# The gate of the first dense layer computed as m(2t - m) on DVE, its high part written by ScalarE

## The chip, the cores and the metric

The kernel runs on one core of a Trainium2 chip. The metric is device time in microseconds (us) of one execution. The engines are called as in the profile: PE (TensorE, matmul), PEld (its weight loads), DVE (VectorE), ACT (ScalarE), POOL (GpSimd) and SP (SyncE, which issues all DMAs of this kernel). Each takes its instructions in a fixed order and waits on semaphores for the others.

## The reference, cut to what matters

Attention over 4 batches, 8 heads, 1152 rows and 64 columns, with neighbouring query rows averaged, then two dense layers on its 2304 rows of 512. The first of them has the gate that is changed:

```python
h = x @ w_in                                   # 2304 x 2048
g = np.where(h >= 1, h, np.where(h <= -1, 0.0, (h + 1) ** 2 / 4))
y = g @ w_out                                  # 2304 x 512
```

The second takes the maximum of three products of y and multiplies it by a last matrix. With t = max(0, h/2 + 1/2) and m = min(t, 1) the gate is g = t^2 where t is at most 1, and 2t - 1 above; both kernels use that.

## The kernel before

**Split numbers.** Matmuls run in float16 on pairs: a float32 array is scaled and written as a high part and a low part (what the rounding left), and a product takes three matmuls (high-high, high-low, low-high). Whoever writes a pair writes the high part first and then the low part from the float32 array and the high part. For the gate that is `g[:, 0]` and `g[:, 1]`.

**Units of attention.** The loop goes over 48 units (b, i, p): batch, third of the 576 query rows, pair of heads. A unit has three score tiles ("who" 0, 1, 2): scores `sc` on PE (L352), the maximum `st` on DVE (L366), scale (L367) and exp `pf` on ACT (L368). Tiles 0 and 1 are split into `hl` (ACT L421, DVE L422) and turned by DMA; tile 2 is turned on PE (`tr`, L404) and split from there (ACT L410, DVE L411). PE then multiplies with V (`av`, L440), and DVE scales the sum into `xf` (L453). Batch 0 is done without these splits.

**Loads of attention.** Every second unit loads and prepares the queries of the next two (`q_prep`): a DMA into `qn`, an add on POOL (L321), square and scale, a split (POOL L245, DVE L246), transposes. Around a change of batch the units also prepare K and V of the next batch: squares on ACT (L266), splits `kpre` and `vhl` (POOL L245, then DVE L246 of 128x1152).

**Dense work between.** From unit 6 on every unit also does four steps of `dense_steps`: two tiles of `up_steps` (ph on PE, L506, then the gate) and one of `down_steps` (py on PE, L532). A gate tile is 128x384 float32, that is 128 of the 2048 columns twice for 192 rows; there are 3 x 4 x 8 = 96 of them. A gate tile before:

```python
nc.scalar.activation(out=t2, in_=ph, func=AF.Relu, scale=hh, bias=0.5)             # L511 ACT
# L512 DVE: rl = max(t, 1) - 1        L513 POOL: rl = t + rl
# L514 DVE: t2 = min(t, 1) * rl       L515 POOL: g high = gs * t2
# L517 DVE: g low = gs * t2 - g high
```

PE reads g only after all eight tiles of a (b, i) have been written, so in the loop there is a unit or more between a gate tile and its use. The tiles t2 and rl have two buffers each.

**What sets the order.** During attention PE's order is the one in which the program is written (`tc.manual_schedule`); DVE, ACT, POOL and SP get theirs from the scheduler, which may interleave dense and attention work. After attention (from about 852 us) PE's order too is the scheduler's. There the last gate tiles stand beside the preparation of the second layer's weights (`st_m`, `wm`: DVE L156 to L161, ACT L664, L147), of which POOL does a part once (L672, L673, 128x2304). The second layer follows until the end.

Of the kernel before, what the change touches and what calls it, by code (L numbers as in the profile page):

```python
# [11 lines left out]
AF = mybir.ActivationFunctionType  # L12
ALU = mybir.AluOpType
# [38 lines left out]
def body(ctx: ExitStack, tc: tile.TileContext, q, k, v, w_in, w_out, w1, w2, w3, w_o2, out):  # L52
    nc = tc.nc
# [416 lines left out]
    def scales(b):  # L470
        hu = small.tile([P, 1], F32, tag="hu", name=f"hu{b}")
        hh = small.tile([P, 1], F32, tag="hh", name=f"hh{b}")
        nc.vector.tensor_scalar(out=hu, in0=U_in[:, 1:2], scalar1=Uv[b][:, NPAIR:NPAIR + 1],
                                scalar2=None, op0=ALU.mult)
        nc.vector.tensor_scalar(out=hh, in0=Uv[b][:, NPAIR + 1:NPAIR + 2], scalar1=0.5, scalar2=None, op0=ALU.mult)

        gd = small.tile([P, 1], F32, tag="dgd", name=f"dgd{b}")
        gs = small.tile([P, 1], F32, tag="dgs", name=f"dgs{b}")
        nc.vector.tensor_scalar(out=gd, in0=hu, scalar1=2.0 ** 31, scalar2=1.0, op0=ALU.mult, op1=ALU.max)
        nc.vector.tensor_scalar(out=gd, in0=gd, scalar1=2.0 ** -15, scalar2=None, op0=ALU.mult)  # L480
        nc.vector.reciprocal(out=gs, in_=gd)
        dst[b] = hh, gd, gs
# [3 lines left out]
    def acc(x, name):  # L486
        ps, tag = room[x]
        return ps.tile([P, 512], F32, tag=tag, name=name)

    def up_steps(b, i):  # L490

        if i == 0:
            scales(b)
        hh, gd, gs = dst[b]
        x = xh.pop((b, i))
        g = gp.tile([P, 2, NF, NB], F16, tag="g", name=f"g{b}_{i}")
        gt[b, i] = g
        for f2 in range(NF // 2):
            key = f"{b}_{i}_{f2}"
            fs = slice(2 * f2, 2 * f2 + 2)  # L500
            ph = acc("h", "ph" + key)[:, :2 * NB].rearrange("p (a n) -> p a n", a=2)
            for a in range(2):
                ff = 2 * f2 + a
                for kt in range(KD):
                    for e, (wi, xi) in enumerate(((0, 0), (0, 1), (1, 0))):
                        nc.tensor.matmul(ph[:, a], win[:, wi, kt, ff * P:(ff + 1) * P], x[:, xi, kt],  # L506
                                         start=(kt == 0 and e == 0), stop=(kt == KD - 1 and e == 2))

            t2 = room["t2"].tile([P, 2, NB], F32, tag="t2", bufs=room["n"], name=f"t2_{key}")
            rl = room["t2"].tile([P, 2, NB], F32, tag="rl", bufs=room["n"], name=f"rl_{key}")  # L510
            nc.scalar.activation(out=t2, in_=ph, func=AF.Relu, scale=hh, bias=0.5)  # L511
            nc.vector.tensor_scalar(out=rl, in0=t2, scalar1=1.0, scalar2=-1.0, op0=ALU.max, op1=ALU.add)  # L512
            nc.gpsimd.tensor_tensor(out=rl, in0=t2, in1=rl, op=ALU.add)  # L513
            nc.vector.scalar_tensor_tensor(out=t2, in0=t2, scalar=1.0, in1=rl, op0=ALU.min, op1=ALU.mult)  # L514
            nc.gpsimd.tensor_scalar(out=g[:, 0, fs, :], in0=t2, scalar1=gs, scalar2=1.0,  # L515
                                    op0=ALU.mult, op1=ALU.mult)
            nc.vector.scalar_tensor_tensor(out=g[:, 1, fs, :], in0=t2, scalar=gs, in1=g[:, 0, fs, :],  # L517
                                           op0=ALU.mult, op1=ALU.subtract)
            yield
# [20 lines left out]
    def dense_steps(units):  # L540

        down = iter(())
        for b, i in units:
            for k, _ in enumerate(up_steps(b, i)):
                yield
                if k % 2 == 1:
                    next(down, None)
                    yield
                    yield
            down = down_steps(b, i)  # L550
        for _ in down:
            yield
            yield
# [299 lines left out]
```

## Time and profile before

| | before |
|---|---|
| time, median of 2 runs | 1233.24 us (1231.83 to 1234.66) |
| time of the profiled execution | 1239.84 us |
| its span | 1237.9 us |
| busy: PE, DVE, ACT, POOL | 1077.9, 857.5, 696.8, 302.9 us |
| POOL L513 and L515 (the gate) | 103.7 and 70.7 us, 96 instructions each |
| chain that ended last: PE, DVE, POOL, DMA | 41%, 17%, 4%, 7% of the span |

The page has five parts that are read here: busy time by engine, 40 slices of the span, the chain of waits that ended last, groups of instructions by line, and DMA issues. By the slices the run has five stretches: up to about 170 us weights and the first batch, without dense work; to 300 us the rest of batch 0; to 840 us attention with dense work; to 950 us the end of the first dense layer beside the next layer's weights; then the second layer, in which PE is full (283 of 288 us) and nothing of the gate runs.

### The profile page before, as it was taken

What the parts mean: (1) busy time and instruction counts of PE and PEld (TensorE: products, weight loads), DVE (VectorE), ACT (ScalarE), POOL (GpSimd) and SP (SyncE); (2) the same over time, 40 slices, a digit from 0 to 9 for tenths busy, and PEclk for the clock granted to TensorE, in tenths of its full rate; (3) what the DMA queues carried; (4) which work ended last, traced back from release to release, by engine and by line L of the source; (5) the groups of instructions that cost most, each with busy time, mean ns of one, the idle gap of its engine ahead of it and who ended that gap; (6) DMA issues with size and microseconds to landing.
All of it is one profiled execution on the core that took longest, in us unless ns stands there. A gap on an engine that the chain in (4) does not pass through costs nothing.

```text
span 1237.9 us, 26735 instructions
## 1 busy us (share of the span) xinstructions
PE 1077.9 (87%) x11058; PEld 881.2 (71%) x11058; DVE 857.5 (69%) x1454; ACT 696.8 (56%) x1241; POOL 302.9 (24%) x306
## 2 busy tenths in 40 slices
PE   0456788899999987999988899998697999999998
PEld 0334567677788876888877788887696876767774
DVE  3988765657888888988888988886988652322220
ACT  3868676656667777667776677766453411122111
POOL 1310012323222344322234422221643020100000
PEclk9867889999999999999999999999899999999999
DMA  9963211446766688965588766547433220000001
GB/s 289 267 199 106 90 27 26 84 87 155 129 113 120 109 172 170 167 110 110 110 158 177 146 105 107 97 88 157 160 96 117 90 67 18 10 27 18 17 18 43
DMA packets 273753, 134.90 MB, mean 109 GB/s; under 512 B 229088, under 2 KB 256736, under 8 KB 272608
## 3 DMA queue, kind: packets, MB, share of 16 engines
q1 hardware_dynamic: 273632, 133.20, 48.5%
q8 instruction: 86, 1.41, 0.5%
q14 instruction: 35, 0.29, 0.1%
HBM read 62.39 MB, written 9.44 MB: 58 GB/s over the span
## 4 chain that ended last, share of the span: by engine, by line
PE 41%; DVE 17%; issue 7%; DMA 7%; ACT 6%; POOL 4%; SPq 2%; ACTq 0%; POOLq 0%; DVEq 0%
PE p L752 17%; PE po L769 5%; PE ph L506 5%; PE py L532 4%; DVE st L366 4%; DMA qn<-in_q_dram 3%; PE sc L352 3%; PE tr L404 3%; PE av L440 2%; DVE g L517 2%; DVE hl L422 2%; DVE t L514 2%; ACT pf L368 1%; POOL g L515 1%; ACT hl L421 1%
## 5 line engine op out<-in xcount | busy, mean ns | idle before, releaser
L352 PE MATMUL sc<-kst,qst 128*64 128x512 f16 (+3 forms) x1152 | 178.2, 347 | 62.6 <-DMA qst<-qpre 21.1
L532 PE MATMUL py<-g,wou 128*128 128x192 f16 x2304 | 201.1, 248 | 22.4 <-POOL g L515 7.8
L752 PE MATMUL p<-yh,wm 128*128 128x288 f16 x1728 | 216.0, 287 | 3.7 <-ACT py L536 2.7
L532 PEld LDWEIGHTS <-wou 128*128 128x128 f16 x2304 | 191.3, 99 | 31.8 <-issue 31.4
L506 PE MATMUL ph<-xh,win 128*128 128x192 f16 x2304 | 203.2, 249 | 4.9 <-ACT py L536 2.6
L366 DVE TENSOR_REDUCE st<-sc 128x1 f32<-128x1152 f32 x144 | 194.1, 1348 | 18.0 <-PE sc L352 17.8
L752 PEld LDWEIGHTS <-wm 128*128 128x128 f16 x1728 | 169.6, 98 | 49.6 <-issue 4.4
L506 PEld LDWEIGHTS <-win 128*128 128x128 f16 x2304 | 195.1, 99 | 7.5 <-issue 5.7
L368 ACT ACTIVATE pf<-sc,st,esc 128x1152 f32<-128x1152 f32 x144 | 188.7, 1311 | 4.5
L352 PEld LDWEIGHTS <-qst 128*64 128x64 f16 (+1 forms) x1152 | 85.6, 109 | 124.3 <-issue 56.9
L513 POOL TENSOR_TENSOR rl<-t,rl 128x384 f32<-128x384 f32 x96 | 103.7, 1083 | 185.3 <-DVE rl L512 185.3
L404 PE MATMUL tr<-ident,pf 128*128 128x128 f32 x648 | 98.9, 306 | 26.3 <-ACT pf L368 17.4
L422 DVE TENSOR_TENSOR hl<-pf,hl 128x1152 f16<-128x1152 f32 x72 | 104.3, 1449 | 22.7 <-ACT hl L421 22.6
L404 PEld LDWEIGHTS tr<-ident,pf 128*128 128x128 f32 x648 | 83.5, 161 | 40.9 <-ACT pf L368 24.8
L367 ACT ACTIVATE st<-st,esc 128x1 f32<-128x1 f32 x144 | 41.6, 289 | 119.0 <-DVE st L366 118.8
L760 ACT ACTIVATE h<-mx 128x288 f16<-128x288 f32 x48 | 21.2, 442 | 133.3 <-DVE mx L758 133.3
L757 DVE TENSOR_TENSOR mx<-p,mx 128x288 f32<-128x288 f32 x48 | 21.9, 456 | 106.3 <-PE p L752 105.7
L515 POOL TENSOR_SCALAR g<-t,dgs 128x384 f16<-128x384 f32 x96 | 70.7, 738 | 97.0 <-DVE t L514 91.4
L440 PE MATMUL av<-pt,vhl 128*64 128x192 f16 x1944 | 87.1, 247 | 2.7 <-DMA pt<-hl 2.7
L440 PEld LDWEIGHTS <-vhl 128*64 128x64 f16 x1944 | 79.3, 110 | 12.4 <-issue 8.5
L517 DVE SCALAR_TENSOR_TENSOR g<-t,dgs,g 128x384 f16<-128x384 f32 x96 | 74.2, 781 | 16.4 <-POOL g L515 16.2
L421 ACT ACTIVATE hl<-pf 128x1152 f16<-128x1152 f32 x72 | 83.4, 1159 | 0.9
(169 smaller groups left out, 1339.0 us busy)
## 6 DMA issues: line engine op xcount, KB each, us to landing
kn<-in_k_dram SPq DMA_DIRECT2D x16, 576.0 KB, 4.6
vn<-in_v_dram SPq DMA_DIRECT2D x16, 576.0 KB, 5.0
raw_m<-in_moe_w_dram SPq DMA_DIRECT2D x12, 768.0 KB, 5.1
raw_in<-in_moe_w_in_dram SPq DMA_DIRECT2D x8, 1024.0 KB, 5.4
qn<-in_q_dram SPq DMA_DIRECT2D x24, 256.0 KB, 4.0
raw_ou<-in_moe_w_out_dram SPq DMA_DIRECT2D x10, 512.0 KB, 4.6
qst<-qst SPq DMA_DIRECT2D x48, 96.0 KB, 2.2
y_d<-ys SPq DMA_DIRECT2D x48, 96.0 KB, 2.0
```

The source lines that it names most:

```text
L352: nc.tensor.matmul(sc[m0:m1, n0:n1], qst[b, i, p][who][:, var, m0:m1], ks[:, h, n0:n1], start=(var == 0), stop=(var == 1))
L366: nc.vector.tensor_reduce(out=m, in_=sc, axis=AX.X, op=ALU.max, negate=True)
L368: nc.scalar.activation(out=pf, in_=sc, func=AF.Exp, bias=nb, scale=e, accum_out=sums[b, i, p][:, who:who + 1])
L404: nc.tensor.transpose(tr[:, c * P:(c + 1) * P], pf[:, c * P:(c + 1) * P], ident)
L421: nc.scalar.activation(out=hl[:, 0], in_=pf, func=AF.Copy)
L422: nc.vector.tensor_tensor(out=hl[:, 1], in0=pf, in1=hl[:, 0], op=ALU.subtract)
L440: nc.tensor.matmul(acc[64 * h:64 * h + 64], vhl[b, p][:, vi, h, c, :], pt[:, h, pi * KT + c, :], start=(c == 0 and e == 0), stop=(c == KT ...
L506: nc.tensor.matmul(ph[:, a], win[:, wi, kt, ff * P:(ff + 1) * P], x[:, xi, kt], start=(kt == 0 and e == 0), stop=(kt == KD - 1 and e == 2))
L513: nc.gpsimd.tensor_tensor(out=rl, in0=t2, in1=rl, op=ALU.add)
L517: nc.vector.scalar_tensor_tensor(out=g[:, 1, fs, :], in0=t2, scalar=gs, in1=g[:, 0, fs, :], op0=ALU.mult, op1=ALU.subtract)
L532: nc.tensor.matmul(py, wou[:, ff // 2, wi, ff % 2, m * P:(m + 1) * P], g[:, gi, ff, :], start=(ff == 0 and e == 0), stop=(ff == NF - 1 and ...
L752: nc.tensor.matmul(ph[:, :NB2], wm[:, wi, i, kt, ff * P:(ff + 1) * P], yh[:, yi, kt, n0:n0 + NB2], start=(kt == 0 and e == 0), stop=(kt == ...
```

## The change

The gate becomes m(2t - m) with m = min(t, 1). DVE forms m from t (one operation, L512), 2t - m (L513, new on DVE) and the product (L514, now a plain tensor-tensor product). The high part of g is written by ACT instead of POOL. DVE's low part is the same instruction as before. Lines behind the gate stand one line earlier in the changed kernel: its L515 is the high part, its L516 the low part, which was L517.

```diff
-            nc.vector.tensor_scalar(out=rl, in0=t2, scalar1=1.0, scalar2=-1.0, op0=ALU.max, op1=ALU.add)
-            nc.gpsimd.tensor_tensor(out=rl, in0=t2, in1=rl, op=ALU.add)
-            nc.vector.scalar_tensor_tensor(out=t2, in0=t2, scalar=1.0, in1=rl, op0=ALU.min, op1=ALU.mult)
-            nc.gpsimd.tensor_scalar(out=g[:, 0, fs, :], in0=t2, scalar1=gs, scalar2=1.0,
-                                    op0=ALU.mult, op1=ALU.mult)
+            nc.vector.tensor_scalar(out=rl, in0=t2, scalar1=1.0, scalar2=None, op0=ALU.min)
+            nc.vector.scalar_tensor_tensor(out=t2, in0=t2, scalar=2.0, in1=rl, op0=ALU.mult, op1=ALU.subtract)
+            nc.vector.tensor_tensor(out=t2, in0=t2, in1=rl, op=ALU.mult)
+            nc.scalar.activation(out=g[:, 0, fs, :], in_=t2, func=AF.Copy, scale=gs)
             nc.vector.scalar_tensor_tensor(out=g[:, 1, fs, :], in0=t2, scalar=gs, in1=g[:, 0, fs, :],
                                            op0=ALU.mult, op1=ALU.subtract)
```

The scheduler places the new instructions. The first place is one unit of batch 3 without loads, (3, 1, 3), about 783 to 798 us of the profile. DVE before, from the first gate tile's first operation to the third score tile's maximum (`st_1_3_2`); `t_3_0_2` and `t_3_0_3` are the unit's two gate tiles, `st_1_3_1` is the second maximum:

```order
L512 TENSOR_SCALAR rl_0_2_10770<-t_3_0_2_10769 128x384
L422 TENSOR_TENSOR hl_1_3_0_10832<-pf_1_3_0_10728,hl_1_3_0_10832 128x1152
L514 SCALAR_TENSOR_TENSOR t_3_0_2_10769<-t_3_0_2_10769,rl_0_2_10770 128x384
L512 TENSOR_SCALAR rl_0_3_10803<-t_3_0_3_10802 128x384
L366 TENSOR_REDUCE st_1_3_1_10826<-sc_1_3_1_10819 128x1
L517 SCALAR_TENSOR_TENSOR g_0_10493<-t_3_0_2_10769,dgs_10489,g_0_10493 128x384
L514 SCALAR_TENSOR_TENSOR t_3_0_3_10802<-t_3_0_3_10802,rl_0_3_10803 128x384
L453 SCALAR_TENSOR_TENSOR xf_1_10363<-av_1_2_10836,Uv_9317,R_1_2_10810 128x192
L366 TENSOR_REDUCE st_1_3_2_10905<-sc_1_3_2_10892 128x1
```

and of the change, between the same two:

```order
L512 TENSOR_SCALAR rl_0_2_10770<-t_3_0_2_10769 128x384
L513 SCALAR_TENSOR_TENSOR t_3_0_2_10769<-t_3_0_2_10769,rl_0_2_10770 128x384
L422 TENSOR_TENSOR hl_1_3_0_10832<-pf_1_3_0_10728,hl_1_3_0_10832 128x1152
L514 TENSOR_TENSOR t_3_0_2_10769<-t_3_0_2_10769,rl_0_2_10770 128x384
L512 TENSOR_SCALAR rl_0_3_10803<-t_3_0_3_10802 128x384
L366 TENSOR_REDUCE st_1_3_1_10826<-sc_1_3_1_10819 128x1
L513 SCALAR_TENSOR_TENSOR t_3_0_3_10802<-t_3_0_3_10802,rl_0_3_10803 128x384
L516 SCALAR_TENSOR_TENSOR g_0_10493<-t_3_0_2_10769,dgs_10489,g_0_10493 128x384
L453 SCALAR_TENSOR_TENSOR xf_1_10363<-av_1_2_10836,Uv_9317,R_1_2_10810 128x192
L514 TENSOR_TENSOR t_3_0_3_10802<-t_3_0_3_10802,rl_0_3_10803 128x384
L366 TENSOR_REDUCE st_1_3_2_10905<-sc_1_3_2_10892 128x1
```

The new 2t - m stands ahead of `hl` for the first tile, and between the two maxima for the second, where now four instructions stand instead of three. ACT of the change in the same unit, from the last of `R` to the third exp (before, ACT had these rows without the two L515):

```order
L388 ACTIVATE R_1_2_10810<-tr_1_2_2_10732 64x64
L515 ACTIVATE g_0_10493<-t_3_0_2_10769,dgs_10489 128x384
L367 ACTIVATE st_1_3_1_10826<-st_1_3_1_10826,esc_1_3_10717 128x1
L368 ACTIVATE pf_1_3_1_10827,sm_1_3_10727<-sc_1_3_1_10819,st_1_3_1_10826,esc_1_3_10717 128x1152
L421 ACTIVATE hl_1_3_1_10910<-pf_1_3_1_10827 128x1152
L515 ACTIVATE g_0_10493<-t_3_0_3_10802,dgs_10489 128x384
L367 ACTIVATE st_1_3_2_10905<-st_1_3_2_10905,esc_1_3_10717 128x1
L368 ACTIVATE pf_1_3_2_10906,sm_1_3_10727<-sc_1_3_2_10892,st_1_3_2_10905,esc_1_3_10717 128x1152
```

The two L515 are new there; the second stands ahead of the scale and exp of the third score tile. The second place is POOL in a unit that loads queries (about 362 to 376 us); before, from the split of one query tile to the second high part:

```order
L245 TENSOR_SCALAR qpre_2_2_4978<-qn_2_2_4974,sqq_2_2_4979 128x6x64
L513 TENSOR_TENSOR rl_2_6_3758<-t_0_2_6_3757,rl_2_6_3758 128x384
L321 TENSOR_TENSOR qn_0_2_6100<-qn_0_2_6100 128x6x64
L515 TENSOR_SCALAR g_2_2955<-t_0_2_6_3757,dgs_1149 128x384
L513 TENSOR_TENSOR rl_2_7_3791<-t_0_2_7_3790,rl_2_7_3791 128x384
L515 TENSOR_SCALAR g_2_2955<-t_0_2_7_3790,dgs_1149 128x384
```

and of the change, around the same two rows (`qpre_2_2_4978`, `qn_0_2_6100`):

```order
L321 TENSOR_TENSOR qn_0_0_5546<-qn_0_0_5546 128x6x64
L245 TENSOR_SCALAR xh_0_3627<-xf_0_2832,Uv_2833 128x768
L245 TENSOR_SCALAR qpre_2_2_4978<-qn_2_2_4974,sqq_2_2_4979 128x6x64
L321 TENSOR_TENSOR qn_0_2_6100<-qn_0_2_6100 128x6x64
L245 TENSOR_SCALAR qpre_0_0_5550<-qn_0_0_5546,sqq_0_0_5551 128x6x64
L321 TENSOR_TENSOR qn_1_0_6620<-qn_1_0_6620 128x6x64
```

Before, the high part of one gate tile and both operations of the next stood behind the load's add, L321; in the change no gate row is left there, and only the loads' own rows and `xh`, the split that feeds ph, follow each other. The third place is POOL after attention, before:

```order
L515 TENSOR_SCALAR g_1_11532<-t_3_1_5_12187,dgs_10489 128x384
L513 TENSOR_TENSOR rl_1_6_12281<-t_3_1_6_12280,rl_1_6_12281 128x384
L513 TENSOR_TENSOR rl_1_7_12321<-t_3_1_7_12320,rl_1_7_12321 128x384
L672 TENSOR_SCALAR st_m_12154<-st_m_12154,s_m 128x2304
L515 TENSOR_SCALAR g_1_11532<-t_3_1_6_12280,dgs_10489 128x384
L673 TENSOR_TENSOR wm<-st_m_12154,wm 128x3x768
L515 TENSOR_SCALAR g_1_11532<-t_3_1_7_12320,dgs_10489 128x384
```

and of the change:

```order
L245 TENSOR_SCALAR xh_0_10111<-xf_0_9316,Uv_9317 128x768
L245 TENSOR_SCALAR qpre_2_2_11439<-qn_2_2_11435,sqq_2_2_11440 128x6x64
L245 TENSOR_SCALAR xh_1_11159<-xf_1_10363,Uv_9317 128x768
L245 TENSOR_SCALAR xh_2_12085<-xf_2_11411,Uv_9317 128x768
L671 TENSOR_SCALAR st_m_12154<-st_m_12154,s_m 128x2304
L672 TENSOR_TENSOR wm<-st_m_12154,wm 128x3x768
L722 TENSOR_SCALAR yh_13173<-yf_0_13174,ysc_13171 128x576 x2
```

The two wide operations stay on POOL, one line earlier in number, and no part of the gate stands behind them.

## Rows read from the trace of the kernel before

**Rows 1.** Busy time by stretch: start:end, length, then busy time of each engine.

```profile
core 0: us, PE busy (x) PEld busy (x) DVE busy (x) ACT busy (x) POOL busy (x), PEclk, DMA share, GB/s
300.00:720.00 420.00, 384.41 (x4776) 335.92 (x4776) 363.22 (x595) 293.22 (x542) 147.28 (x153) 0.99 0.74 140
840.00:950.00 110.00, 88.15 (x1032) 83.41 (x1030) 92.15 (x138) 55.64 (x93) 46.55 (x34) 0.93 0.43 129
```

**Rows 2.** Sums of the same view: seven units that load queries, then seven without loads.

```profile
sum 113.00, PE 104.44 PEld 91.09 DVE 95.92 ACT 73.78 POOL 36.90; mean PE 14.92 PEld 13.01 DVE 13.70 ACT 10.54 POOL 5.27
...
sum 102.10, PE 101.68 PEld 89.55 DVE 86.84 ACT 76.43 POOL 25.58; mean PE 14.53 PEld 12.79 DVE 12.41 ACT 10.92 POOL 3.65
```

**Rows 3.** Instructions of the gate's tiles, all: duration ns min/median/max, first and last start.

```profile
L512 DVE TENSOR_SCALAR rl<-t x96: 341/354/1184, 173.9 to 937.6; 128x384 f32<-128x384 f32 x96
L514 DVE SCALAR_TENSOR_TENSOR t<-t,rl x96: 541/546/1340, 177.4 to 939.7; 128x384 f32<-128x384 f32 x96
...
L517 DVE SCALAR_TENSOR_TENSOR g<-t,dgs,g x96: 601/613/4896, 180.9 to 941.1; 128x384 f16<-128x384 f32 x96
```

**Rows 4.** DVE by line, 300 to 720 us: busy us, mean ns, idle before and releaser.

```profile
L422 DVE TENSOR_TENSOR hl<-pf,hl 128x1152 f16<-128x1152 f32 x51 | 73.4, 1440 | 15.8 <-ACT hl L421 15.7
L517 DVE SCALAR_TENSOR_TENSOR g<-t,dgs,g 128x384 f16<-128x384 f32 x51 | 37.6, 747 | 9.6 <-POOL g L515 9.4
L514 DVE SCALAR_TENSOR_TENSOR t<-t,rl 128x384 f32<-128x384 f32 x52 | 31.2, 606 | 2.8 <-POOL rl L513 2.8
L512 DVE TENSOR_SCALAR rl<-t 128x384 f32<-128x384 f32 x52 | 21.6, 416 | 10.8 <-ACT t L511 10.7
L246 DVE SCALAR_TENSOR_TENSOR vhl<-vn,sb,vhl 128x1152 f16<-128x1152 f32 x9 | 16.8, 1871 | 4.4 <-POOL vhl L245 4.3
L246 DVE SCALAR_TENSOR_TENSOR kpre<-kn,sb,kpre 128x1152 f16<-128x1152 f32 x9 | 12.7, 1415 | 2.4 <-POOL kpre L245 2.3
```

**Rows 5.** Who waited for whom, POOL, 300 to 720 us: total us, times, longest.

```profile
POOL qn L321 <- DMA qn<-in_q_dram: 56.3, 13, 6.9
```

**Rows 6.** POOL and DVE in order of time in a unit with query loads: start, duration.

```profile
370.61 1.00 POOL L321 TENSOR_TENSOR qn<-qn 128x384 f32<-128x384 f32 x1 [2.54 <-DMA qn<-in_q_dram]
371.59 0.58 POOL L515 TENSOR_SCALAR g<-t,dgs 128x384 f16<-128x384 f32 x1
...
372.21 1.34 DVE L517 SCALAR_TENSOR_TENSOR g<-t,dgs,g 128x384 f16<-128x384 f32 x1 [0.91 <-POOL g L515]
```

**Rows 7.** Order of time in the unit without loads, 783 to 798 us.

```profile
790.19 0.55 DVE L514 SCALAR_TENSOR_TENSOR t<-t,rl 128x384 f32<-128x384 f32 x1
790.66 0.35 DVE L512 TENSOR_SCALAR rl<-t 128x384 f32<-128x384 f32 x1
...
793.55 1.34 DVE L366 TENSOR_REDUCE st<-sc 128x1 f32<-128x1152 f32 x1
...
795.34 1.35 DVE L422 TENSOR_TENSOR hl<-pf,hl 128x1152 f16<-128x1152 f32 x1
795.45 1.31 ACT L368 ACTIVATE pf<-sc,st,esc 128x1152 f32<-128x1152 f32 x1
...
797.68 1.15 PE L404 MATMUL tr<-ident,pf 128*128 128x128 f32 x9
```

**Rows 8.** Groups by line, the whole run: busy us, mean ns, idle before, releasers.

```profile
L511 ACT ACTIVATE t<-ph,hh 128x384 f32<-128x384 f32 x96 | 54.9, 574 | 26.3 <-DVE g L517 17.5 <-PE ph L506 4.5 <-DVE u_m L94 2.7
```

**Rows 9.** POOL and DVE in order of time, about 893 us.

```profile
892.20 5.24 POOL L673 TENSOR_TENSOR wm<-st_m,wm 128x2304 f16<-128x2304 f32 x1
...
892.95 4.90 DVE L517 SCALAR_TENSOR_TENSOR g<-t,dgs,g 128x384 f16<-128x384 f32 x1
```

**Rows 10.** DVE by line, 852 to 948 us.

```profile
L517 DVE SCALAR_TENSOR_TENSOR g<-t,dgs,g 128x384 f16<-128x384 f32 x13 | 15.5, 1190 | 1.7 <-POOL g L515 1.7
```

**Rows 11.** Who waited for whom, PE, 840 to 950 us.

```profile
PE py L532 <- POOL g L515: 7.8, 3, 5.4
PE py L532 <- DVE g L517: 7.0, 4, 5.3
```

## The prediction, made before the changed kernel ran

> **What bounds the kernel now.** I read the busy time by stretch first: the share of busy time over the whole run mixes stretches with different limits. Between 300 and 720 us PE works 384.41 of 420 us [rows 1], so 35.6 us are lost there; DVE is next with 363.22, and POOL has 147.28. From 840 to 950 us PE works 88.15 of 110 and loses 21.9 [rows 1]. Only what shortens these losses can show in the time. Behind 950 us the second layer fills PE and no gate runs.
>
> The same view over single units says where the first loss sits. Seven units without loads take 102.10 us with PE busy for 101.68: full, and a faster gate gains nothing there. Seven units that load queries take 113.00 with PE busy for 104.44 [rows 2]. That is 10.9 us more than the plain seven, of which 8.6 are PE standing idle. What is left of the 35.6, that is 27.0, lies in the remaining units, most of them those that prepare K and V.
>
> Then the waits. In that stretch POOL stood 56.3 us, 13 times, for the query DMA before its add [rows 5]; and POOL takes its instructions in order, so a gate operation that is ready stands behind a load that has not come. [Rows 6] show one: the add waits 2.54 us and lasts 1.00, the gate's high part comes behind it, and DVE's low part waits 0.91 for that and then takes 1.34. The groups by line on DVE give 9.4 us of L517 and 2.8 us of L514 waiting for POOL's gate operations [rows 4], together 12.2.
>
> A second effect stands in the durations. The low part's median is 0.613 us [rows 3], its mean between 300 and 720 is 0.747 [rows 4]. Its longest is 4.90, begun at 892.95 beside a POOL operation that runs from 892.20 for 5.24 [rows 9]: both end within half a us of each other (897.44, 897.85), so DVE stood until POOL let go. Operations of DVE with two inputs are lengthened while POOL works.
>
> **What goes: POOL's share.** 96 additions and 96 high parts leave POOL. With them go the waits of 12.2 us on DVE, and part of the lengthening. Of that I count, between 300 and 720, mean less undisturbed duration: L517 51 times 0.134 = 6.8; L514 52 times 0.060 = 3.1; L512 52 times 0.062 = 3.2 [rows 3, 4]; `hl` 51 times 0.09 = 4.6, against the 1.35 of [rows 7]; `vhl` against `kpre`, the same shape, 9 times 0.456 = 4.1 [rows 4]. Sum 21.8. Some is due to POOL's remaining splits and will stay, so 21.8 is an upper end; the lower end is nothing.
>
> **What is added on DVE.** One operation more for each tile: 2t - m and a product replace the one L514. Both are 128x384 float32 with two inputs. No plain product of this shape and no 2t - m is in the trace; L514, same shape and operands, takes 0.546, between 0.354 (L512, one input) and 0.613 (L517) [rows 3]. I take L514's for both. Followed by the next instruction an operation costs less than its duration: L514 starts at 790.19, L512 at 790.66 [rows 7], a step of 0.47. So 52 times 0.47 = 24.4 us between 300 and 720 (by the bounds, 15 to 29, taking steps of 0.28 and 0.55). The minimum instead of maximum and addition stays at L512's 0.354. DVE's balance there: 24.4 - 21.8 - 12.2 = -9.6.
>
> The Trainium skill, page "SBUF — State Buffer", section "Who interferes with whom", says that a DVE instruction with two SBUF inputs contends with a GpSimd instruction that reads SBUF, and that whichever starts first holds the shared ports while the other is blocked; the trace agrees, with 4.90 beside 5.24.
>
> **What is added on ACT.** 96 high parts. ACT's L511 has this shape and takes 0.574 [rows 8]; a third of the exp's 1.31 [rows 7] gives 0.44 as the lower end, the whole exp the upper. I take 0.574: 52 of them are 30 us on an engine that is busy for 293.22 of 420 [rows 1], so ACT does not fill. What counts is the place. In the unit of the first excerpt of the order the second high part stands ahead of the third exp, but that exp waits for the third maximum, which takes DVE 1.34 [rows 7], begins right after the product that the high part needs, and covers its 0.57. So the only addition to the chain from the second maximum by the third to the exp and PE's `tr` is the one DVE operation more between the maxima, 0.47 or less. That exp starts at 795.45 and ends at 796.76, `tr` begins at 797.68 [rows 7]: 0.92 of slack, enough. If the cover were gone, the price is the rival below.
>
> **The sum.** *300 to 720:* the two ways to count it agree: DVE's balance is -9.6, and the seven query units are 10.9 longer than plain ones. I do not add the two, since the waits of the one make the length of the other; with a little from the K and V units I take -12. *720 to 840:* PE is full in the plain units; nothing. *840 to 950:* the 13 low parts take 15.5 us [rows 10] instead of 13 times 0.613 = 8.0; of the 7.5 above it, 4.90 - 0.613 = 4.3 lie under POOL's wide operation [rows 9], which stays, so 3.2 go, while 13 times 0.47 = 6.1 come: DVE loses 2.9. PE's 7.8 us of waiting for POOL's high part go; of the 7.0 for DVE's low part 5.3 are one wait [rows 11], under the same wide operation, and stay. -7.8 + 2.9 = about -5. *170 to 300:* 14 tiles in batch 0, which has no `hl` splits; 14 times 0.47 = 6.6 come and waits on POOL of unknown size go. I take nothing, within 3 either way. Sum -17.
>
> The profiled execution took 1239.84 us (span 1237.9), 6.6 more than the median of the runs, 1233.24. So 1223 for an execution like the profiled one, and 1233.24 - 17 = 1216 for the median.
>
> **The rivals.** *The whole loss comes back.* With POOL nearly free, loads are prepared as they land. Then the query units become plain ones (10.9), some 10 of the 27.0 idle in the other units go as well, and after attention all of PE's waiting for g goes, 14.8 - 2.9 = 11.9. Together 33: 1200 us. For it speaks that 56.3 us of POOL's waiting had the gate in its queue [rows 5]; against it that `vhl`, `kpre` and the wide operation stay on POOL, and that DVE, at 363.22 of 420 [rows 1], is given at most 9.6 of room.
>
> *No gain.* The waits only change their name: the low part waits for ACT as it did for POOL, since ACT too is in order and the high part stands behind an exp of 1.31 or, in K and V units, behind squares. If the 12.2 come back, DVE's balance is +2.6 in 300 to 720, and only the -5 after attention is left: 1228 to 1233.
>
> *Slower.* One chain: all three additions lie between the second maximum and `tr`, 0.47 for 2t - m, 0.47 for the product, and the high part's 0.57 uncovered, as when ACT gets to it only as the third maximum ends. 1.5 less the slack of 0.92 is 0.6 in each of some 36 units of 15 us from 300 to 840 us: +21. With 5 left after attention and half of the query units' gain, 5: 1233 + 21 - 10 = 1244. It decides as soon as more than 0.92 is added on that chain.
>
> *The lock the other way.* [Rows 9] leave open who holds whom: a DVE operation that has begun may hold POOL as well. The new two-input operations would then make POOL's splits late: 18 of K and V [rows 4], by 0.546 each, +9.8, against the -17: 1226. The Trainium skill's page named above states this direction too, in the same section; no row of [rows 9] shows it.
>
> *That the change does not do what it says* is out: in the order no gate row is left on POOL.
>
> **How the numbers follow.** The forecast, 1208.6 to 1224, has 0.55; the whole loss 0.24; no gain 0.11; the lock the other way 0.06; slower 0.04. The predicted time is the likeliest, 1216. The range runs from the middle of the first rival, 1200 (half of its chance lies below, 0.12), past no gain to 1236, and leaves out the slower case; about 0.84 lie in it. A measurement of this kernel tells about 2% from no change: below 1208.6 and above 1257.9. Faster by over 2%: 0.24 of the first rival and the edge of the forecast, 0.26; slower by over 2%: 0.04 with the chain's addition larger than I took it; within: 0.70.
>
> **What would show it.** POOL's busy time falls by the gate's 174.4 to some 128, ACT's rises by 96 times 0.574 to some 752, DVE's by about 10 (+96 x 0.47 or 0.55, less the lengthening). The low part's mean comes near 0.613 and `hl` near 1.35 between 300 and 720; the seven query units take 102 to 104, not 113; the plain units still 102 with PE full; after attention PE's wait for POOL's g is gone and the one beside POOL's wide operation is still there. I am wrong if plain units grow (the chain), if a wait of DVE's low part for ACT takes POOL's place, or if query units stay at 113 with POOL free of the gate, for then their loss was the DMA's or the transposes' and not the queue's.

## The result, and the profile after

| | before | changed |
|---|---|---|
| time, median of 2 runs each | 1233.24 us (1231.83 to 1234.66) | 1215.74 us (1215.64 to 1215.83) |
| ratio to before | | 0.987, 95% interval 0.984 to 0.989 |
| span of the profiled execution | 1237.9 us | 1214.0 us |
| busy: PE, DVE, ACT, POOL | 1077.9, 857.5, 696.8, 302.9 us | 1074.9, 877.9, 745.1, 130.8 us |

The changed kernel is 17.5 us faster. The two profiled executions lie 23.9 us apart, 6.4 more than the medians; most of that belongs to the one execution of before, as a second trace of the same kernel shows (first experiment).

To see where the time went, the run is cut at the same points of the program in each trace: at the first score maximum of a unit, and at the first matmul of the second layer. The units are counted from 0. Busy time by stretch, as in [rows 1], from unit 13 to unit 39 and from unit 47, the last, to the second layer; this second stretch is called "after attention" below. The kernel before:

```profile
300.90:725.30 424.40, 388.81 (x4823) 339.65 (x4822) 366.67 (x605) 296.97 (x552) 146.94 (x154) 0.99 0.73 138
841.50:948.10 106.60, 85.73 (x1015) 81.81 (x1014) 89.20 (x132) 53.78 (x86) 44.65 (x33) 0.94 0.44 132
```

The same two stretches of its second trace:

```profile
292.90:718.70 425.80, 388.67 (x4823) 339.36 (x4821) 366.76 (x605) 297.13 (x552) 148.49 (x154) 0.99 0.72 138
834.80:941.00 106.20, 85.56 (x1014) 81.81 (x1013) 89.14 (x132) 53.48 (x86) 44.60 (x33) 0.94 0.45 132
```

And of the changed kernel:

```profile
291.10:710.40 419.30, 392.57 (x4832) 344.31 (x4831) 382.98 (x662) 323.68 (x604) 53.59 (x49) 0.98 0.70 140
826.30:923.00 96.70, 84.02 (x994) 79.69 (x993) 84.18 (x143) 57.67 (x90) 15.84 (x5) 0.96 0.47 143
```

In attention with dense work (the longer stretch) the change gains 5.1 us against the first trace of before and 6.5 against the second. After attention it gains 9.9 and 9.5. There PE's order is the scheduler's, and the changed kernel has some 20 matmuls fewer ahead of that cut (994 against 1015); with the second layer added, from unit 47 to the end, the gain is 8.6 and 10.0 (396.3 and 397.7 us before, 387.7 after). Between the two stretches PE is full in both kernels. DVE is the engine to look at in the longer one: it is busy 16.3 us more and idle 21.4 less (57.7 before, 36.3 after).

DVE of the changed kernel by line from 290 to 707 us, which holds as many low parts and `hl` as [rows 4] and is to be read beside them (unit 39 begins at 710.4); L513 is the new 2t - m, L516 was L517:

```profile
L422 DVE TENSOR_TENSOR hl<-pf,hl 128x1152 f16<-128x1152 f32 x51 | 70.5, 1383 | 5.2 <-ACT hl L421 3.5
...
L516 DVE SCALAR_TENSOR_TENSOR g<-t,dgs,g 128x384 f16<-128x384 f32 x51 | 32.5, 638 | 1.6 <-ACT g L515 1.6
L513 DVE SCALAR_TENSOR_TENSOR t<-t,rl 128x384 f32<-128x384 f32 x52 | 32.5, 625 | 0.8
L514 DVE TENSOR_TENSOR t<-t,rl 128x384 f32<-128x384 f32 x52 | 31.4, 603 | 0.1
L512 DVE TENSOR_SCALAR rl<-t 128x384 f32<-128x384 f32 x52 | 21.7, 418 | 10.4 <-ACT t L511 10.2
L246 DVE SCALAR_TENSOR_TENSOR kpre<-kn,sb,kpre 128x1152 f16<-128x1152 f32 x9 | 12.7, 1410 | 1.4 <-POOL kpre L245 1.4
L246 DVE SCALAR_TENSOR_TENSOR vhl<-vn,sb,vhl 128x1152 f16<-128x1152 f32 x9 | 12.7, 1410 | 0.1
```

The low part's mean is 0.638 instead of 0.747, `hl` 1.383 instead of 1.440, `vhl` 1.410 instead of 1.871. The 12.2 us of waiting for POOL's gate operations are 1.6 of waiting for ACT. And `hl`, which stood 15.8 us idle for ACT's half of it, stands 5.2: by the order shown with the change, the new operation lies ahead of it and fills that gap.

### The profile page after: what moved, and what is told of

The parts are those of the page before. It is cut to its first block, busy times and chain, and to the rows that moved or that the text cites. A ratio compares the mean times of both kernels' runs of the same rounds, so it can differ in the third digit from the quotient of the medians.

```text
span 1214.0 us, 26619 instructions
## 1 busy us (share of the span) xinstructions
PE 1074.9 (89%) x11058; PEld 881.4 (73%) x11058; DVE 877.9 (72%) x1550; ACT 745.1 (61%) x1337; POOL 130.8 (11%) x114
## 5 line engine op out<-in xcount | busy, mean ns | idle before, releaser
L531 PE MATMUL py<-g,wou 128*128 128x192 f16 x2304 | 203.9, 249 | 15.0 <-DVE xf L453 5.9
L751 PE MATMUL p<-yh,wm 128*128 128x288 f16 x1728 | 215.2, 286 | 1.3 <-DVE yh L724 0.7
L422 DVE TENSOR_TENSOR hl<-pf,hl 128x1152 f16<-128x1152 f32 x72 | 99.0, 1375 | 6.2 <-ACT hl L421 3.5
L515 ACT ACTIVATE g<-t,dgs 128x384 f16<-128x384 f32 x96 | 57.9, 608 | 43.1 <-DVE t L514 43.0
L421 ACT ACTIVATE hl<-pf 128x1152 f16<-128x1152 f32 x72 | 83.4, 1158 | 0.8
L768 PE MATMUL po<-wo,h 128*128 128x512 f16 x288 | 64.3, 379 | 0.0
L516 DVE SCALAR_TENSOR_TENSOR g<-t,dgs,g 128x384 f16<-128x384 f32 x96 | 61.6, 647 | 2.2 <-ACT g L515 2.1
```

The lines of the kernel that those rows point to most:

```text
L421: nc.scalar.activation(out=hl[:, 0], in_=pf, func=AF.Copy)
L422: nc.vector.tensor_tensor(out=hl[:, 1], in0=pf, in1=hl[:, 0], op=ALU.subtract)
L531: nc.tensor.matmul(py, wou[:, ff // 2, wi, ff % 2, m * P:(m + 1) * P], g[:, gi, ff, :], start=(ff == 0 and e == 0), stop=(ff == NF - 1 and ...
L751: nc.tensor.matmul(ph[:, :NB2], wm[:, wi, i, kt, ff * P:(ff + 1) * P], yh[:, yi, kt, n0:n0 + NB2], start=(kt == 0 and e == 0), stop=(kt == ...
L768: nc.tensor.matmul(po, h2t[b][:, hi, ff, t * P:(t + 1) * P], wo[:, wi, ff, :], start=(ff == 0 and e == 0), stop=(ff == NF2 - 1 and e == 2))
```

## The experiments

Each kernel was timed beside the kernel before on the same chip, and its ratio is to that. The experiments ran on several chips, on which the median of the kernel before lay between 1233.2 and 1236.2 us; so a difference in us between two changed kernels is good to some 3 us.

**The kernel before again.** No edit; a second trace.

> The kernel before once more, for a second trace of it. Its first trace had a span of 1237.9 us, the median of its runs is 1233. If the 6 us between them belong to that one execution, this trace shows a span of about 1232 and the stretch from 217 to 301 us, where the granted clock was 0.94 against 1.00 in the changed kernel, is shorter by some 4 us. If the low clock there belongs to the kernel, the stretch is again 83 us at 0.94.

It took 1234.48 us with a span of 1232.5. The stretch from unit 9 to unit 13 took 79.2 us at a granted clock of 1.00, where the first trace has 83.4 at 0.94; from unit 13 on the two traces agree within 1.4 us in each stretch shown above. So the low clock in batch 0 belongs to the first execution, and the changed kernel's 77.2 us there are a gain of 2 at most.

**Only the high part moved to ACT.**

```diff
-            nc.gpsimd.tensor_scalar(out=g[:, 0, fs, :], in0=t2, scalar1=gs, scalar2=1.0,
-                                    op0=ALU.mult, op1=ALU.mult)
+            nc.scalar.activation(out=g[:, 0, fs, :], in_=t2, func=AF.Copy, scale=gs)
```

> The kernel before with only the gate's high part moved from GpSimd to ScalarE; t + max(t,1) - 1 stays on GpSimd, and DVE gets nothing new. Theory 1 (the gate stands in GpSimd's queue behind loads, and that is the price): the addition still stands there, so DVE's product waits for it where the low part waited before; half of the change's gain at most, 1222 to 1229 us. Theory 2 (what counts is GpSimd's busy time beside DVE): 71 of the 174 us go and DVE has no extra operation, so the gain is as large as the change's or larger: 1212 to 1218.

1229.5 us, ratio 0.994 (0.993 to 0.996): less than half of the gain, as the first theory said, and half a us beyond its range. From unit 47 to the second layer it needs 104.8 us, nearly as long as before: one addition of the gate is still behind the two wide operations in POOL's queue, and PE waits for the low part of its tile.

**Only the gate on DVE**, the high part left on POOL.

```diff
-            nc.scalar.activation(out=g[:, 0, fs, :], in_=t2, func=AF.Copy, scale=gs)
+            nc.gpsimd.tensor_scalar(out=g[:, 0, fs, :], in0=t2, scalar1=gs, scalar2=1.0,
+                                    op0=ALU.mult, op1=ALU.mult)
```

> The change with its high part left on GpSimd: m(2t - m) on DVE, one DVE operation more than before, and one GpSimd operation for each gate tile instead of two. Theory 1: the high part still stands behind the queries' add, the low part on DVE waits for it as before, and the query units keep most of their 11 us; with 24 us of DVE added, 1230 to 1242. Theory 2: 104 of 174 us of GpSimd go: 1220 to 1226.

1218.97 us (1215.63 to 1225.81), ratio 0.987 (0.984 to 0.991). That cannot be told from the whole change, although the high part still stands behind the queries' add in POOL's queue; the 1230 to 1242 of the first theory are out. Units 13 to 39 took 417.3 us, 2.0 less than in the changed kernel, and yet the low part waits for POOL there as long as both waits of [rows 4] together (12.2 us):

```profile
DVE g L517 <- POOL g L515: 12.3, 12, 4.1
```

After attention it took 103.6, 6.9 more, with PE waiting there:

```profile
PE py L532 <- POOL g L515: 10.5, 2, 7.1
```

**POOL kept busy for nobody.** The changed kernel with two operations like those that were taken away; nothing reads their result.

```diff
+            nc.gpsimd.tensor_tensor(out=jl, in0=rl, in1=rl, op=ALU.add)
+            nc.gpsimd.tensor_scalar(out=jl, in0=rl, scalar1=gs, scalar2=1.0, op0=ALU.mult, op1=ALU.mult)
```

> The changed kernel with two operations on GpSimd for each gate tile, of the kinds and size that the change took away, that read m and whose result nobody uses; so no instruction of DVE or ScalarE waits for GpSimd more than in the changed kernel, but GpSimd is as busy as before. Theory A (a third of the gain is that DVE's operations are no longer lengthened beside GpSimd): DVE's hl and low part go back to means of 1.44 and about 0.75 between 300 and 720, 1219 to 1225 us. Theory B (only the waits counted): 1214 to 1217.

1257.65 us, ratio 1.017 (1.013 to 1.022): 42 us more than the changed kernel and slower than before, more than either theory gave. Over the whole run DVE is busy 925.1 us instead of 877.9 with the same 1550 instructions. The waits for POOL's useful work grew little: DVE waits 8.9 us for `kpre` instead of 6.6, and PE 3.6 for `yh`, the second layer's input, where it did not wait for it in the changed kernel. The six units from unit 27 to 33, which load queries but no K or V, show best what waits and what lengthening do there. For each of four kernels stand first its waits (PE's `tr` for the exp, DVE for POOL), where it has them, then `hl` and the low part of DVE by line. The kernel before, second trace, 92.7 us:

```profile
PE tr L404 <- ACT pf L368: 4.3, 4, 1.7
DVE g L517 <- POOL g L515: 2.1, 3, 1.8
...
DVE t L514 <- POOL rl L513: 1.2, 1, 1.2
```

```profile
L422 DVE TENSOR_TENSOR hl<-pf,hl 128x1152 f16<-128x1152 f32 x12 | 17.2, 1433 | 4.2 <-ACT hl L421 4.2
...
L517 DVE SCALAR_TENSOR_TENSOR g<-t,dgs,g 128x384 f16<-128x384 f32 x12 | 8.6, 732 | 2.1 <-POOL g L515 2.1
```

Only the gate on DVE, 88.2 us:

```profile
DVE g L517 <- POOL g L515: 1.9, 2, 1.5
...
PE tr L404 <- ACT pf L368: 0.6, 1, 0.6
```

```profile
L422 DVE TENSOR_TENSOR hl<-pf,hl 128x1152 f16<-128x1152 f32 x12 | 16.2, 1354 | 0.6
...
L517 DVE SCALAR_TENSOR_TENSOR g<-t,dgs,g 128x384 f16<-128x384 f32 x12 | 7.3, 610 | 1.9 <-POOL g L515 1.9
```

The changed kernel, 88.2 us:

```profile
PE tr L404 <- ACT pf L368: 0.7, 2, 0.5
```

```profile
L422 DVE TENSOR_TENSOR hl<-pf,hl 128x1152 f16<-128x1152 f32 x12 | 16.3, 1356 | 0.6
...
L516 DVE SCALAR_TENSOR_TENSOR g<-t,dgs,g 128x384 f16<-128x384 f32 x12 | 7.3, 610 | 0.0
```

The changed kernel with POOL kept busy, 91.7 us:

```profile
PE tr L404 <- ACT pf L368: 4.1, 4, 1.5
```

```profile
L422 DVE TENSOR_TENSOR hl<-pf,hl 128x1152 f16<-128x1152 f32 x12 | 18.0, 1501 | 0.6
...
L519 DVE SCALAR_TENSOR_TENSOR g<-t,dgs,g 128x384 f16<-128x384 f32 x12 | 9.1, 762 | 0.0
```

With the gate alone on DVE the low part waits 1.9 us for POOL, about as long as before (2.1; the product's 1.2 is gone), and PE loses only 0.6. With the idle work on POOL no gate operation of DVE waits for POOL, but its operations are long again, and PE loses 4.1 as before. So in these units PE's loss goes with the lengthening, and the low part's wait alone does not bring it. The Trainium skill, page "SBUF — State Buffer", section "Who interferes with whom", names the contention of a DVE instruction with two SBUF inputs and a GpSimd instruction that reads; the trace agrees, with 0.762 against 0.610.

**POOL writing only.** The changed kernel with three memsets of m in place of those two operations, after DVE's last use of it.

```diff
+            for _ in range(3):
+                nc.gpsimd.memset(rl, 0.0)
```

> The changed kernel with three memsets of the gate tile's m on GpSimd, after DVE's last use of it: GpSimd writes and reads nothing, again with nobody waiting for it. The two operations that read cost 42 us. If it is GpSimd's reading that lengthens DVE's operations with two inputs, these keep 0.55, 0.61 and 1.36: 1215 to 1222 us. If any work of GpSimd does it: 1235 to 1260.

1221.23 us, ratio 0.989 (0.986 to 0.992), some 5 us above the changed kernel where the reading operations cost 42. Between 300 and 720 us, POOL's memsets and DVE's operations with two inputs:

```profile
L516 POOL MEMSET rl<- 128x384 f32 x159 | 68.3, 430 | 147.3 <-DVE t L514 141.3
```

```profile
L422 DVE TENSOR_TENSOR hl<-pf,hl 128x1152 f16<-128x1152 f32 x52 | 71.6, 1378 | 5.0 <-ACT hl L421 3.4
...
L518 DVE SCALAR_TENSOR_TENSOR g<-t,dgs,g 128x384 f16<-128x384 f32 x53 | 34.5, 650 | 1.5 <-ACT g L517 1.5
```

Another 68 us of POOL leave DVE's durations where the changed kernel has them (1.383 and 0.638). Units 13 to 39 took 419.4 us, as in the changed kernel; the 5 us lie after attention (101.0 instead of 96.7). The memsets come behind the product, the reading operations behind the minimum, so the place differs as well as the kind. But the same trace holds both kinds: of DVE's instructions from 300 to 720 us, those that run beside a memset alone take 0.606 (low part, 10 of them) and 1.353 (`hl`, 16), those with POOL idle 0.608 and 1.353, and those beside POOL's splits and adds, which read, 1.054 and 1.514 (5 and 8).

**One operation more on DVE.**

```diff
             nc.vector.tensor_scalar(out=rl, in0=t2, scalar1=1.0, scalar2=None, op0=ALU.min)
+            nc.vector.tensor_tensor(out=rl, in0=rl, in1=rl, op=ALU.max)
```

> The changed kernel with one operation more on DVE for each gate tile, max(m, m), right behind the minimum: two inputs, 128x384, and m is as before. It prices what the change added on DVE. If the plain units have the slack of 0.92 us that the trace of before shows, of which the change used some 0.3 to 0.45, another 0.47 stays within it and only the ten units that load K and V pay, 20 times 0.47 = 9: 1221 to 1227 us. If the slack is used up, the other 26 units of attention with dense work pay up to 0.94 each as well: 1235 to 1250.

1231.34 us, ratio 0.997 (0.995 to 0.999): 15.6 more than the changed kernel, between the two expectations. Units 13 to 39 took 429.5 us, 10.2 more, and the eight units behind them 117.2 instead of 115.9, with PE busy 116.70. So the plain units have slack for nearly all of one operation more, and the loaded ones pay. After attention it took 100.3 instead of 96.7, and the second layer 4.1 more, though no gate runs there: 30 more of the run's matmuls stand behind that cut (2147 against 2117), and the granted clock was 0.99 against 1.00; how much belongs to which stays open. Up to unit 13 it was 4.1 us shorter.

**No wide operation on POOL.** The changed kernel with the second layer's first rows of weights done as the others, high part on ACT and low part on DVE.

```diff
-            if kt == 0:
...
-            else:
+            if True:
                 split_rows(wm[:, 0, :, kt, :], wm[:, 1, :, kt, :], st, s[:, kt:kt + 1])
```

> The changed kernel with the two wide operations of the second layer's weights (128x2304, GpSimd L671 and L672) done as for the other three rows of the weights, high part on ScalarE and low part on DVE. In the changed kernel DVE's minimum stands for 4.27 us beside the second of them and PE waits 3.7 us for DVE's low part there. Theory (what was left of the loss after attention is that blocking): the 4.27 becomes 0.35, DVE gets 2.6 us for the low part instead, 1211 to 1214 us. Rival (the wait is only the length of DVE's own work there, 84 of 97 us): 1215 to 1218.

1211.13 us (1207.83 to 1211.34), ratio 0.980 (0.977 to 0.983). From unit 47 to the second layer it takes 92.3 us instead of 96.7, and all gate operations there have their short durations, the minimum 0.352 on the mean instead of 0.631. It beats both kernels: its interval lies, by little, below that of the changed one. PE's wait for the low part did not fall (3.8 us), so the gain goes with the sum of DVE's work there (80.7 instead of 84.2), not with that wait.

**2t - m as max(h, t), from PSUM.**

```diff
-            nc.vector.tensor_scalar(out=rl, in0=t2, scalar1=1.0, scalar2=None, op0=ALU.min)
-            nc.vector.scalar_tensor_tensor(out=t2, in0=t2, scalar=2.0, in1=rl, op0=ALU.mult, op1=ALU.subtract)
-            nc.vector.tensor_tensor(out=t2, in0=t2, in1=rl, op=ALU.mult)
+            nc.vector.scalar_tensor_tensor(out=rl, in0=ph, scalar=hw, in1=t2, op0=ALU.mult, op1=ALU.max)
+            nc.vector.scalar_tensor_tensor(out=t2, in0=t2, scalar=1.0, in1=rl, op0=ALU.min, op1=ALU.mult)
```

> The changed kernel with 2t - m formed as max(h, t) straight from the product in PSUM: two DVE operations ahead of the high part instead of three. Theory (where PE stands idle between 300 and 720 us DVE's work is the limit): DVE loses 96 times about 0.3 us, 16 us of it between 300 and 720, of which PE's 23 us of idle time in the units that load K and V give back 3 to 7: 1209 to 1213 us. Rival (PSUM's bank is held until DVE comes to it, and PE waits for the bank): 1217 to 1225.

1213.11 us, ratio 0.982 (0.979 to 0.986), at the end of what the first theory gave; the interval overlaps that of the changed kernel (0.984 to 0.989). Units 13 to 39 took 417.3 us, 2.0 less, but the gain does not lie where the theory put it. The two groups of six units in which K and V are loaded, from unit 21 and from unit 33:

```profile
411.80:516.80 105.00, 92.22 (x1128) 80.53 (x1127) 92.40 (x167) 79.03 (x151) 17.30 (x16) 0.98 0.82 166
604.30:709.30 105.00, 94.06 (x1131) 82.42 (x1129) 92.04 (x166) 78.71 (x149) 17.30 (x15) 0.97 0.77 154
```

They took 210.0 us, as in the changed kernel (210.2), with 8.3 us less work on DVE.

**Both of these.**

> The changed kernel with max(h, t) from PSUM and without the two wide operations on GpSimd, that is the two gains (2.6 and 4.6 us) in one kernel. They lie in different stages (300 to 720 us and after attention), so they should add: 1206 to 1210 us. If both only shorten DVE's work after attention: 1209 to 1212.

1211.96 us, ratio 0.982 (0.979 to 0.985). The gains did not add here. After attention it took 93.0 us, near the 92.3 without the wide operations, but units 13 to 39 took 421.0, 3.7 more than with max(h, t) alone, though nothing of those units differs in the code. Most of it lies in the six units from 21, to be read beside the first row of the last view:

```profile
412.60:520.60 108.00, 96.37 (x1128) 83.84 (x1126) 92.32 (x166) 78.93 (x150) 17.45 (x15) 0.94 0.81 160
```

They took 3.0 us more; PE is busy 4.1 us longer over as many matmuls (1128), at a granted clock of 0.94 instead of 0.98. So that part is the clock of PE and not the gate; whether it belongs to this one execution stays open.

**Three tries at the wait alone.** The kernel before, with its gate, and the query loads earlier: first with the tile's two buffers, then with three, then with three and the add held until the unit's first maximum. The core of the edits:

```diff
             if n % 2 == 1 and n + 1 < len(units):
                 q_prep(*units[n + 1])
+            elif n % 2 == 0 and n >= 12 and n + 2 < len(units):
+                q_load(*units[n + 2])
...
+            nc.vector.scalar_tensor_tensor(out=x, in0=late_q[b, i, p], scalar=0.0, in1=x, op0=ALU.mult, op1=ALU.add)
```

> The kernel before with each query load issued one unit earlier, so that GpSimd's add finds its data; the gate is untouched, and the order on GpSimd is that of before. Theory 1: GpSimd's wait for the query DMA (56 us between 300 and 720) goes, the query units between 528 and 620 us lose their 4.3 us of PE idle and those between 301 and 424 a part of their 6.5; 1222 to 1228. Theory 2 (GpSimd's busy time lengthens DVE's operations, the queue costs nothing): the wait goes and the time stays at 1231 to 1235.

1237.54 us, ratio 1.001 (0.999 to 1.003). The load did not move: with both buffers held it stands at the same place in SP's order.

> The kernel before with each query load a unit earlier and three buffers for it, and the add free to go where the scheduler puts it, which is a unit earlier too. If the add still waits for its load (it did for 50 us between 300 and 720 in the kernel before), the time is that of before, 1231 to 1238 us. If the wait is gone and it was the price of the query units, PE's idle time from 528 us on falls from 4.3 below 1 us and the whole to 1222 to 1229.

1236.46 us, ratio 1.002 (1.000 to 1.004). The load moved two units earlier, into the place of the load before it, and the add moved with it, so that it waited for its load as before (45.3 us between 300 and 720).

> The kernel before with three buffers for the query tiles, each load one unit earlier, and GpSimd's add held until the first score tile's maximum of the unit, when the data has landed (one DVE operation of one column for every second unit does that). The gate is untouched: its operations on GpSimd wait for no load, but GpSimd and DVE run beside each other as before. Theory A: half of the query units' loss stays, 1230 to 1234 us, with PE idle in the six units from 528 us on at 2 to 4 us of 4.3. Theory B (the loss of the query units is the wait behind the load): PE's idle time there falls below 1 us and the whole to 1222 to 1229.

1268.23 us, ratio 1.027 (1.024 to 1.031). The add waited for no load any more, but then the turned query tiles came late: from unit 13 to 21 PE waited 16.2 us for them. None of the three takes the wait away and leaves the rest, so what the wait behind the load costs by itself was not measured directly. What bounds it is the kernel with only the gate on DVE, whose low part waits as long as before and whose units 13 to 39 are no longer than those of the changed kernel.

## Why the prediction was right, and which of its terms were not

The time, 1215.74 us, lies 0.3 us from the forecast of 1216, and the sum of -17 from the measured -17.5. That the sum fits so closely is chance: the term for 300 to 720 us was twice too large and the one for after attention half of what was measured, and the two errors cancel.

**300 to 720 us: forecast -12, measured -5.1 to -6.5.** By the list of [rows 2] the query units did what was forecast. The same seven as in [rows 2], and then the same seven without loads, in the changed kernel:

```profile
sum 103.18, PE 100.21 PEld 87.49 DVE 97.79 ACT 80.12 POOL 12.17; mean PE 14.32 PEld 12.50 DVE 13.97 ACT 11.45 POOL 1.74
...
sum 103.70, PE 102.76 PEld 90.62 DVE 91.32 ACT 83.13 POOL 4.55; mean PE 14.68 PEld 12.95 DVE 13.05 ACT 11.88 POOL 0.65
```

113.00 became 103.18, within the 102 to 104 that was said. But part of that only moved across the cuts, since DVE's maxima shifted against PE's work: the plain ones grew from 102.10 to 103.70, and unit 14, which stands in neither list, from 14.6 to 16.7. All fourteen units without K and V loads (13 to 20 and 27 to 32) took 215.2 us before and take 209.1 now. That is -6.1, where the forecast counted 9.6 to 10.9; PE's idle time in them fell from 10.9 to 4.2:

```profile
sum 215.20, PE 204.35 PEld 178.58 DVE 183.57 ACT 149.73 POOL 62.59; mean PE 102.17 PEld 89.29 DVE 91.78 ACT 74.86 POOL 31.29
...
sum 209.10, PE 204.93 PEld 179.90 DVE 190.25 ACT 164.73 POOL 17.71; mean PE 102.46 PEld 89.95 DVE 95.12 ACT 82.36 POOL 8.86
```

That plain units grow was a sign of being wrong, by the chain to `tr`. The eight units from 39 show that it is not that: they took 115.9 us instead of 116.2, with PE full in both.

What failed too is the "little from the K and V units". The two groups of six units from 21 and from 33, before:

```profile
423.50:528.00 104.50, 92.27 (x1125) 80.64 (x1124) 91.70 (x165) 73.63 (x136) 42.10 (x40) 0.98 0.84 166
620.60:725.30 104.70, 92.20 (x1124) 80.42 (x1123) 91.41 (x164) 73.62 (x136) 42.25 (x40) 0.98 0.79 155
sum 209.20, PE 184.46 PEld 161.07 DVE 183.10 ACT 147.24 POOL 84.35; mean PE 92.23 PEld 80.53 DVE 91.55 ACT 73.62 POOL 42.17
```

And in the changed kernel:

```profile
412.00:518.00 106.00, 93.11 (x1128) 81.61 (x1127) 96.33 (x178) 79.64 (x150) 18.05 (x16) 0.97 0.77 164
606.20:710.40 104.20, 94.53 (x1130) 82.80 (x1128) 96.40 (x178) 79.31 (x150) 17.82 (x15) 0.95 0.75 155
sum 210.20, PE 187.64 PEld 164.41 DVE 192.73 ACT 158.95 POOL 35.88; mean PE 93.82 PEld 82.20 DVE 96.36 ACT 79.47 POOL 17.94
```

They gained nothing (0.7 against the second trace of before, 210.9). PE's idle time fell a little, from 24.7 to 22.6, but PE took 3.2 us longer over nearly the same matmuls, at a granted clock of 0.97 and 0.95 instead of 0.98. DVE's work there rose by 9.6 to 192.73 of 210.20 us. That this is what holds them is not shown: one operation more on DVE costs the two groups 4.4 us (107.8 and 106.8), but with max(h, t), which takes 8.3 us of DVE's work away again, they took 210.0. Why PE's idle time there did not fall further, and whether the lower clock belongs to the changed kernel, stays open.

**DVE's balance.** The relief was counted as 21.8 at its upper end, and taken whole: L512's 3.2 and L514's 3.1 did not come (0.418 and 0.603 after, 0.416 and 0.606 before, though L514 is another instruction now), L517 gave 5.6 of 6.8, `hl` 2.9 of 4.6, `vhl` all 4.1: 12.6. The step of one operation was right where nothing disturbs it (the new one takes 0.55 to 0.56 us); on the mean it takes 0.625, or 0.55 without the 0.08 by which the next one overlaps it, so 28.6 were added and not 24.4. What the balance lacked is that an operation put ahead of `hl` fills a gap in which DVE waited for ACT: 10.6 us of the added 28.6 cost nothing. With the measured terms, 28.6 - 12.6 - 10.6 and the waits' 10.6 (12.2 less 1.6), the balance is -5.2, near the 5.1 that the stretch gained; the -9.6 had errors of opposite sign in it.

**The reason given for the query units.** The prediction put the waits of 12.2 us first, as work queued behind a load. The runs put the lengthening first: with the gate alone on DVE the low part still waits (12.3 us in units 13 to 39, 1.9 in the six units) and PE loses no more than in the changed kernel, and in the six units PE loses its 4 us again where only the lengthening is back. So the place was right, and the first of the two reasons given for it was not.

**After attention: forecast -5, measured -9.5 to -9.9.** The wait for POOL's high part went, as said. The mis-sized term is DVE's, forecast at +2.9: its busy time there fell by 5.0. Only the gate's own low parts were counted as relieved; the weights' operations beside them were lengthened too. DVE by line in that stretch, before:

```profile
L517 DVE SCALAR_TENSOR_TENSOR g<-t,dgs,g 128x384 f16<-128x384 f32 x14 | 16.1, 1151 | 1.7 <-POOL g L515 1.7
L159 DVE SCALAR_TENSOR_TENSOR st_m<-raw_m,st_m 128x768 uint32<-128x768 uint32 x12 | 13.6, 1134 | 0.0
...
L156 DVE TENSOR_SCALAR st_m<-st_m 128x768 f32<-128x768 f32 x12 | 8.4, 713 | 6.7 <-ACT st_m L155 6.7
...
L512 DVE TENSOR_SCALAR rl<-t 128x384 f32<-128x384 f32 x14 | 4.8, 350 | 1.0 <-ACT t L511 1.0
```

And after:

```profile
L159 DVE SCALAR_TENSOR_TENSOR st_m<-raw_m,st_m 128x768 uint32<-128x768 uint32 x12 | 11.4, 949 | 0.0
...
L516 DVE SCALAR_TENSOR_TENSOR g<-t,dgs,g 128x384 f16<-128x384 f32 x14 | 10.3, 760 | 0.5 <-ACT g L515 0.5
L512 DVE TENSOR_SCALAR rl<-t 128x384 f32<-128x384 f32 x14 | 8.7, 631 | 0.7 <-ACT t L511 0.7
...
L156 DVE TENSOR_SCALAR st_m<-st_m 128x768 f32<-128x768 f32 x12 | 6.6, 553 | 5.5 <-ACT st_m L155 5.5
```

L159 and L156 alone give 4.0 us back, the low parts 5.8. That the wide operation would still hold DVE was right, but another instruction stands there now, and the wait of 5.3 us for the low part, which was to stay, did not. What PE waits for in this stretch after the change, beside [rows 11]:

```profile
PE py L531 <- DVE g L516: 3.7, 5, 2.1
...
PE py L531 <- ACT g L515: 2.3, 2, 1.4
```

**170 to 300 us and 720 to 840 us: forecast nothing.** Against the second trace of before, units 6 to 13 took 125.8 us instead of 125.9, and units 39 to 47 115.9 instead of 116.1.

**The rivals.** *The whole loss comes back*: it did not; the K and V units still lose 22.6 us of PE, and of the 14.8 us in which PE waited for g after attention 6.0 are left. *Slower*, by the chain to `tr`: it did not come, PE is busy for all of 710.4 to 826.3 us; with one operation more PE is busy 116.70 of 117.2 there, so the slack is nearly used. *No gain*: the low part waits 1.6 us for ACT, so the wait did not change its name. *The lock the other way*: it exists, as the rows at the end show, but not where the rival priced it: DVE waited 1.4 us for `kpre` and 0.1 for `vhl` (before 2.4 and 4.4). POOL's busy time, 130.8, and ACT's, 745.1, are near the 128 and 752 that were forecast; DVE's rose by 20 and not by 10, the relief having been counted too high.

## What to carry to other kernels

Work on GpSimd has a price beyond its own queue where it reads while DVE has operations with two inputs beside it: here two small operations for each tile, for whose results nobody waits, cost 42 us. So the gain of taking an operation away from GpSimd is looked for in the means of DVE's other lines against their medians, all of them, not only the changed ones, and an operation added on DVE is weighed by the gaps it falls into, not by its duration alone. Units that are cut out by one engine's events shift against another engine's work, so a gain is counted over all units of a stretch, not over a chosen list, and with the granted clock of each beside it.

## What the runs showed of the hardware

The holding goes both ways, and it also meets an operation of DVE with one input. POOL and DVE of the changed kernel, in order of time:

```profile
868.61 6.84 POOL L671 TENSOR_SCALAR st_m<-st_m,s_m 128x2304 f32<-128x2304 f32 x1 [10.53 <-ACT wm L670]
...
872.88 2.98 DVE L516 SCALAR_TENSOR_TENSOR g<-t,dgs,g 128x384 f16<-128x384 f32 x2
...
875.53 4.74 POOL L672 TENSOR_TENSOR wm<-st_m,wm 128x2304 f16<-128x2304 f32 x1
...
876.22 4.27 DVE L512 TENSOR_SCALAR rl<-t 128x384 f32<-128x384 f32 x1
```

The same wide multiplication took POOL 3.28 us before; here it took 6.84. Up to 873.5 DVE ran eight operations with two inputs one behind the other beside it, all at their usual length. The next one, the second of the two low parts in the second row, took 2.45 us instead of 0.61 and ended at 875.86, 0.4 behind the multiplication. Then the minimum, one input and 0.35 us long, stood for 4.27 us and ended at 880.49, 0.2 us behind POOL's wide subtraction. The Trainium skill, page "SBUF — State Buffer", section "Who interferes with whom", counts `tensor_scalar` from SBUF among the operations that can take the shared ports; the trace agrees.
